# Reordering the start and the chunk loop of a fused attention, expert and dense kernel on one core: an early `w_out` slab, two-chunk turns, lagging rests and a softmax in four parts

## The chip, the core and the metric

The kernel runs on one core of a Trainium2 chip. TensorE multiplies matrices into PSUM banks, VectorE, ScalarE and GpSimd (POOL) work on tiles in SBUF (VectorE and ScalarE on PSUM too), and SyncE issues the transfers from and to HBM. Each engine runs its own instructions in their order and waits for the others by semaphores. The metric is the device time of one execution in microseconds; the number to predict is the median of the runs of the changed kernel. The kernel before took 355.84 us (median of three; 353.69 to 357.73).

## The reference

Three stages on 3072 tokens of width 512. The expert weights, `w_in` and `w_out` come as below; `w_in` and `w_out` are 64-bit floats in memory, which the kernel turns to 32-bit ones on the chip ("decoding").

```python
# 1. decayed linear attention in blocks, 8 heads of 64
intra = (q k^T * D) v;  inter = (q * lam_pow) kv_state;  out = intra + inter
# 2. soft mixture of experts: 32 slots, 8 experts of 4 slots
d = softmax(x @ phi, over tokens);  slot_input = d.T @ x
slot_out[e] = relu(slot_input[e] @ w1[e]) @ w2[e]
c = softmax(x @ phi, over slots);   x = c @ slot_out
# 3. dense stage, 512 -> 2048 -> 512
h = x @ w_in;  g = h - tanh(h);  return g @ w_out
```

## The kernel before, in words

**Attention and routing (to about 129 us).** A loop over 24 units (6 blocks of 128 positions, 4 batches) computes scores, values, the running state and the routing logits. Weight loads run beside it: `fill` (L171) issues the next half slab on SyncE whenever its ring has a free place. The rings are pools of 1 MB places: `a` has 3, `b` 12, `d` and `e` one each, `c` 4 (`RING`, L61). The letter of each of the 32 expert slabs stands in `RING_OF` (L62); all 16 slabs of `w_in` (`wi0` to `wi7`) and `w_out` (`wo0` to `wo7`) go to `a`, in the order wi0, wi1, wo0, wo1, wi2, wi3, wo2, wo3 and so on (`slabs`, L166). `freed` (L183) gives a place back when the last instruction that reads the slab has been issued.

**Experts (129 to 171 us).** For each expert `expert1` (L569) multiplies the slot inputs by w1, `expert_t` (L583) turns the result and VectorE copies it to `hz`, `expert2` (L595) of the expert before multiplies by w2. Among them the softmax over slots is made in two halves: `gate` (L625) turns the logits, `gate_v` (L632) does the softmax on VectorE and ScalarE, `parts` (L651) splits it in a rounded part and a rest; `gate_t` (L665) makes the six column blocks `c4`.

**Dense stage.** Because x = c @ slot_out has rank 32, h comes from M = slot_out @ w_in: `make_m(m)` (L729) makes the 512 columns of M that two `wi` slabs give, `put_m` (L739) lays them out as `ms` (TensorE, a ScalarE copy, a VectorE subtraction on 32 rows), `turn_m` (L749) gives `mt` with the mean of each column (TensorE, a VectorE copy). Both use one PSUM bank (7), except the first ones. There are 6 column blocks c of 512 tokens and 16 row blocks f of 128 features, so 96 chunks (c, f). For each chunk `d_of` (L773) multiplies on TensorE into one of three banks; `r_of` (L779) squares d on ScalarE into `s` and multiplies: on VectorE from PSUM (L790), or, for the chunks in `POOL_R` (L56), on POOL after a second ScalarE pass `e`. The result `r`, the "rest", stands for the cubic part of h - tanh(h). `product` (L794) multiplies the four 128-token parts of r by the rounded `w_out` block `wr` (`round_wo`, L759, ScalarE) and adds up over the f of a turn in four banks. `TURNS` (L51) lists the turns (c, first f, end f). `keep` (L800) empties the banks: at a first turn of c into `part` on ScalarE, at the second by a VectorE addition and a store. The first-order part of the result, a product of c4 with `qc`, comes from `linear_1` to `linear_3` (L822 to L869), which need all of M and of w_out; the second turn of each c adds it in its banks (L1014), except for c = 0 (`LATE`, L55), for which `late_linear` (L809) does it a chunk or more later by itself.

**Order.** The order is written out by hand. `decode_ops` (L102) makes a slab's three VectorE steps (L107, L110, L113), each on 1024 elements a partition for a 1 MB slab. The steps of `wi0` and `wi1` stand ahead of everything (L699); those of the other 14 slabs form the list `filler`, and in iteration n of the chunk loop (L983) `FILLER[n]` of them are issued, after `d_of(n + 3)` and `r_of(n + 3)` and ahead of the products of chunk n. In turns the products of the last two chunks are issued together. When a slab is done, `decoded` (L961) puts what follows on later iterations, by `DUE` (L58): `make_m` 1, `put_m` and `turn_m` 2, `round_wo` 2 iterations later. Before the loop stand `make_m(0)`, `put_m(0)`, `turn_m(0)`, the d and r of chunks 0 to 2, three steps (`wo0`) and its rounding (L947 to L982). `keep_warm` (L608) issues products whose result nobody reads.

Of the kernel before, what the change touches and what calls it, by code (L numbers as in the profile page):

```python
# [18 lines left out]
P = 128  # L19
# [29 lines left out]
WARM_MAIN = 2, 2  # L49

TURNS = [  # L51
    (0, 0, 4), (1, 0, 4), (2, 0, 4), (3, 0, 8), (4, 0, 8), (5, 0, 12), (0, 4, 16), (1, 4, 16),
    (2, 4, 16), (3, 8, 16), (4, 8, 16), (5, 12, 16),
]
LATE = 0  # L55
POOL_R = range(2, 48, 2)  # L56
FILLER = [3] + [1] * 16 + [1, 1, 0] * 5 + [1] * 20
DUE = 1, 2, 2  # L58
# [3 lines left out]
RING_OF = "a" * 3 + "b" * 12 + "de" + "c" * 4 + "a" * 3 + "b" * 7 + "a"  # L62
# [3 lines left out]
def tile_main(ctx, tc, qkv, lam, phi, w1, w2, w_in, w_out, out):  # L66
# [496 lines left out]
    with pool("exp") as ep:  # L563
# [109 lines left out]
        fill()  # L673
        for e in range(NE):
            hr = expert1(e)
            if e in (1, 2):
                parts()
            if e >= 1:
                expert2(e - 1)
            if e < 2:  # L680
                softmax = gate(e)
# [3 lines left out]
            if e < 2:  # L685
                parts = softmax()
# [52 lines left out]
    def put_m(m, bk=None):  # L739
        pp = bank(bk or MISC, [P, 4, P], "pp")  # L740
        for j in range(4):
            nc.tensor.matmul(pp[:, j], put[:, j], m_t[m], start=True, stop=True, skip_group_check=True)
# [4 lines left out]
            out=ms[64:96, sl], in0=pp[64:96], in1=ms[64:96, sl].bitcast(F32), op=ALU.subtract)  # L747

    def turn_m(m, bk=None):  # L749
        tp = bank(bk or MISC, [P, 4, NS + 1], "tp")  # L750
        nc.tensor.matmul(
            tp.rearrange("p j s -> p (j s)"), m_t.pop(m), tsel.rearrange("p j s -> p (j s)"),
            start=True, stop=True)
        nc.vector.tensor_copy(mt[:, 4 * m:4 * m + 4], tp)
        placed.update((2 * m, 2 * m + 1))
# [15 lines left out]
    d_t, r_t = {}, {}  # L771
# [28 lines left out]
    def keep(c, op, t, sl, lo, hi):  # L800
# [5 lines left out]
        if hi == NF and c != LATE:  # L806
            nc.sync.dma_start(out=out_v[c, :, t, sl], in_=pt)

    def late_linear(t):  # L809
        op = bank(MISC, [P, DM], "opl")  # L810
        pt = part_t[LATE][:, t]
        nc.tensor.matmul(op, c4[:, LATE, t * P:(t + 1) * P], qc, start=True, stop=True)
        nc.vector.tensor_tensor(out=pt, in0=op, in1=pt, op=ALU.add)
        nc.sync.dma_start(out=out_v[LATE, :, t], in_=pt)
# [289 lines left out]
```

## Time and profile before

| what | value |
|---|---|
| median of three runs | 355.84 us |
| lowest, highest | 353.69, 357.73 us |
| the profiled execution | 357.14 us, of it 355.3 us span from the first to the last instruction |
| granted TensorE clock, mean | 0.944 of full speed |
| TensorE, VectorE, ScalarE, POOL busy | 313.1, 213.4, 141.1, 116.6 us |
| moved by DMA | 81.06 MB |

Full speed of TensorE's clock is 2.4 GHz; 0.50 is its lower level, 1.2 GHz. TensorE's instructions are pipelined, so its rows overlap and a busy TensorE is not one at its peak; from start to start is the safer reading. "DVE" is VectorE, "ACT" ScalarE, "PE" TensorE, "PEld" its weight loads, "SPq" the queue of SyncE. Times in the profile count from the first instruction.

### The profile page before, as it was taken

How to read it: one execution, taken by the hardware profiler on the slowest of the kernel's cores; microseconds unless marked ns; L12 is line 12 of the kernel's file. 1: busy time of each engine (PE TensorE's matmuls, PEld its weight loads, DVE VectorE, ACT ScalarE, POOL GpSimd, SP SyncE). 2: the span in 40 equal slices, each digit the busy share in tenths (PEclk: the TensorE clock that was granted, in tenths of full speed). 3: DMA queues.
4: the chain of work that ended last, by engine and by line, in shares of the span. 5: the costliest groups of instructions: out<-in, count | busy, mean ns of one | idle time of the engine just before them, and what ended most of it. 6: DMA issues, size and time to landing. Idle time of an engine off the chain costs nothing.

```text
span 355.3 us, 7076 instructions
## 1 busy us (share of the span) xinstructions
PE 313.1 (88%) x2828; PEld 232.6 (65%) x2828; DVE 213.4 (60%) x347; ACT 141.1 (40%) x270; POOL 116.6 (33%) x154
## 2 busy tenths in 40 slices
PE   8499999999999998799837887789788989999993
PEld 8488898989788863344515654566565657787773
DVE  2326555555544336301678989767959598767773
ACT  2023323232323223222136867469457534353330
POOL 6117687759583031110012635135525100000000
PEclk9659999999999999999856999899989999999998
DMA  6858999999999999999636453535300003303324
GB/s 196 285 179 283 400 395 400 391 397 390 390 391 317 366 378 393 400 399 375 240 136 224 159 197 132 176 101 192 124 0 2 2 0 120 118 0 118 120 73 168
DMA packets 34197, 81.06 MB, mean 228 GB/s; under 512 B 3048, under 2 KB 4464, under 8 KB 34160
## 3 DMA queue, kind: packets, MB, share of 16 engines
q1 hardware_dynamic: 34160, 80.56, 61.8%
q8 instruction: 23, 0.38, 0.4%
q14 instruction: 14, 0.11, 0.1%
HBM read 74.25 MB, written 6.30 MB: 227 GB/s over the span
## 4 chain that ended last, share of the span: by engine, by line
PE 34%; DVE 27%; DMA 25%; ACT 5%; issue 4%; POOL 1%; SPq 1%; DVEq 0%; POOLq 0%; ACTq 0%
PE ops L797 11%; DMA qk<-in_qkv 7%; DMA w<-in_w 7%; DVE r L790 6%; DMA k<-in_qkv 5%; DVE part L805 4%; PE dps L777 4%; PE xp L297 3%; DVE wif L110 3%; DVE wif L113 3%; PE sc L278 2%; ACT s L784 2%; DVE wif L107 2%; DMA v<-in_qkv 2%; DMA wi<-in_w_in 2%
## 5 line engine op out<-in xcount | busy, mean ns | idle before, releaser
L797 PE MATMUL ops<-wr,r 128*128 128x512 f32 (+1 forms) x388 | 114.7, 411 | 8.4 <-ACT wr L762 6.4
L797 PEld LDWEIGHTS ops<-wr,r 128*128 128x128 f32 x388 | 74.8, 195 | 34.5 <-ACT wr L762 5.5
L784 ACT ACTIVATE s<-dps 128x512 f32<-128x512 f32 x96 | 56.5, 603 | 55.1 <-PE dps L777 51.6
L790 DVE SCALAR_TENSOR_TENSOR r<-dps,mt,s 128x512 fp32r<-128x512 f32 x73 | 53.8, 747 | 27.0 <-ACT s L784 26.9
L788 POOL TENSOR_TENSOR r<-e,s 128x512 fp32r<-128x512 f32 x23 | 37.5, 1634 | 79.3 <-ACT e L787 62.6
L777 PE MATMUL dps<-c,ms 128*128 128x512 f32 x96 | 40.2, 439 | 7.6 <-DVE r L790 6.6
L282 DVE TENSOR_TENSOR at<-sc,dtab 128x512 f32<-128x512 f32 x48 | 30.8, 686 | 17.1 <-DMA dtab<-zd 8.6
L247 POOL TENSOR_TENSOR qs<-qk,ql 128x512 f32<-128x512 f32 x20 | 25.5, 1273 | 24.2 <-DMA qk<-in_qkv 20.5
L297 PE MATMUL xp<-at,v 128*64 128x128 f32 x384 | 28.6, 291 | 4.6 <-DVE at L282 4.6
L315 DVE TENSOR_TENSOR st<-up,sd 64x256 f32<-64x256 f32 x32 | 13.5, 423 | 29.5 <-PE up L307 29.0
L301 ACT COPY xt<-xp 128x512 f32<-128x512 f32 x24 | 14.1, 586 | 39.3 <-PE xp L297 39.3
L337 ACT COPY xn<-xnp 128x512 f32<-128x512 f32 x24 | 14.1, 586 | 39.3 <-PE xnp L335 39.3
L777 PEld LDWEIGHTS dps<-c,ms 128*128 128x128 f32 x96 | 19.0, 200 | 16.1 <-DVE r L790 9.4
L278 PE MATMUL sc<-qk 64*128 64x128 f32 x384 | 28.8, 291 | 0.7 <-DMA qk<-in_qkv 0.7
L278 PEld LDWEIGHTS sc<-qk 64*128 64x128 f32 x384 | 24.1, 193 | 6.9 <-DMA qk<-in_qkv 3.4
L297 PEld LDWEIGHTS xp<-at,v 128*64 128x64 f32 x384 | 22.2, 143 | 8.2 <-DVE at L282 5.1
L254 POOL TENSOR_TENSOR kc<-k,dtab 128x512 f32<-128x512 f32 x20 | 21.2, 1060 | 18.8 <-PE up L307 11.5
L291 PE MATMUL xp<-qs,st 128*128 128x128 f32 x160 | 21.2, 276 | 0.0
L260 POOL TENSOR_TENSOR sd<-st,ql 64x256 f32<-64x256 f32 x32 | 19.8, 618 | 1.2
L598 PE MATMUL op<-w,hz 128*32 128x512 f32 x128 | 16.5, 595 | 3.5 <-DVE hz L591 3.5
L291 PEld LDWEIGHTS xp<-qs,st 128*128 128x128 f32 x160 | 19.5, 192 | 0.1
L335 PE MATMUL xnp<-cst,xt 128*128 128x128 f32 x96 | 16.2, 292 | 0.0
(188 smaller groups left out, 379.0 us busy)
## 6 DMA issues: line engine op xcount, KB each, us to landing
w<-in_w SPq DMA_DIRECT2D x64, 512.0 KB, 8.8
qk<-in_qkv SPq DMA_DIRECT2D x24, 512.0 KB, 7.8
wi<-in_w_in SPq DMA_DIRECT2D x16, 512.0 KB, 5.0
wo<-in_w_out SPq DMA_DIRECT2D x16, 512.0 KB, 3.4
v<-in_qkv SPq DMA_DIRECT2D x24, 256.0 KB, 6.8
out<-part SPq DMA_DIRECT2D x23, 256.0 KB, 2.2
k<-in_qkv SPq DMA_DIRECT2D x17, 256.0 KB, 8.5
dtab<-zd SPq DMA_DIRECT2D x2, 256.0 KB, 5.0
```

Of the source, the lines that this page charges most:

```text
L247: nc.gpsimd.tensor_tensor(out=qs_t[u], in0=qk_t[u][:, 0], in1=ql, op=ALU.mult)
L254: nc.gpsimd.tensor_tensor(out=kc_t[u], in0=k_t.pop(u).rearrange("p (h d) -> p h d", h=H), in1=kd, op=ALU.mult)
L260: nc.gpsimd.tensor_tensor(out=sd_t[u][sl], in0=st_t[b][sl, :, sl], in1=lb[sl].to_broadcast([DH, NP, DH]), op=ALU.mult)
L278: nc.tensor.matmul(sc[h2][:, p], qk[sl, 1, p], qk[sl, 0, p], start=True, stop=True)
L282: nc.vector.tensor_tensor(out=by_head(at_t[u], h2), in0=sc[h2], in1=by_head(dtab, h2), op=ALU.mult)
L291: nc.tensor.matmul(xp[:, p], st_t[b][:, p], qs_t[u][:, p], start=p == 0, stop=False, skip_group_check=True)
L297: nc.tensor.matmul(xp[h2 * DH:(h2 + 1) * DH, p], v[:, h * DH:(h + 1) * DH], at[:, h], start=c == 0 and p == 0, stop=True, skip_group_check ...
L777: nc.tensor.matmul(d_t[n], ms[:, f * P:(f + 1) * P], c4[:, c], start=True, stop=True)
L784: nc.scalar.activation(out=s, in_=d, func=AF.Square, scale=math.sqrt(1.0 / 3))
L788: nc.gpsimd.tensor_tensor(out=r_t[n], in0=e, in1=s, op=ALU.mult)
L790: nc.vector.scalar_tensor_tensor(out=r_t[n], in0=d, scalar=mt[:, f, NS:], in1=s, op0=ALU.add, op1=ALU.mult)
L797: nc.tensor.matmul(op, r_t[n][:, t * P:(t + 1) * P], wr_t[f // 2][:, f % 2, sl], start=first, stop=last)
```

## The change

- The last expert slab goes to ring `b` instead of `a`.
- The softmax over slots: half 0 is computed behind expert 0 and split behind expert 1, half 1 behind experts 2 and 3. Before, half 0 was computed behind expert 0, half 1 behind expert 1, and each was split behind `expert1` of the next one.
- The first two turns have 2 chunks instead of 4, and their second turns 14 instead of 12.
- The three steps of `wo0` are issued ahead of `turn_m(0)` and `put_m(0)`, `turn_m` comes ahead of `put_m` everywhere (in the loop a chunk ahead), and its rounding ahead of the first d. Two groups of two `keep_warm` products are added.
- `s_of(n + 3)` issues the squares (and `e`) where `r_of(n + 3)` did; the rest itself is `r_of(n + 2)`.
- POOL has the rests of the odd chunks 7 to 45 (20) instead of the even ones 2 to 46 (23).
- `FILLER` is another list: 15 steps in iterations 0 to 10, then three in four iterations, to iteration 42 (before: one in each up to 16, then two in three, then one in each, to iteration 41).
- `late_linear` goes; c = 0 gets its first-order part at the end of its second turn like the others.

```diff
-WARM_MAIN = 2, 2
+WARM_MAIN = 2, 2, 2, 2
 TURNS = [
-    (0, 0, 4), (1, 0, 4), (2, 0, 4), (3, 0, 8), (4, 0, 8), (5, 0, 12), (0, 4, 16), (1, 4, 16),
+    (0, 0, 2), (1, 0, 2), (2, 0, 4), (3, 0, 8), (4, 0, 8), (5, 0, 12), (0, 2, 16), (1, 2, 16),
     (2, 4, 16), (3, 8, 16), (4, 8, 16), (5, 12, 16),
 ]
-LATE = 0
-POOL_R = range(2, 48, 2)
-FILLER = [3] + [1] * 16 + [1, 1, 0] * 5 + [1] * 20
-DUE = 1, 2, 2
+POOL_R = range(7, 47, 2)
+FILLER = [3, 1, 1, 2, 1, 2, 1, 1, 1, 1, 1, 0] + [1, 1, 1, 0] * 8
+DUE = 1, 2, 3, 2
-RING_OF = "a" * 3 + "b" * 12 + "de" + "c" * 4 + "a" * 3 + "b" * 7 + "a"
+RING_OF = "a" * 3 + "b" * 12 + "de" + "c" * 4 + "a" * 3 + "b" * 8
...
+        softmax = []
         for e in range(NE):
             hr = expert1(e)
-            if e in (1, 2):
-                parts()
             if e >= 1:
                 expert2(e - 1)
             if e < 2:
-                softmax = gate(e)
+                softmax.append(gate(e))
...
             expert_t(e, hr)
-            if e < 2:
-                parts = softmax()
+            if e in (0, 2):
+                parts = softmax[e // 2]()
+            elif e in (1, 3):
+                parts()
...
+    def s_of(n):
+        s, e = tmp("s", bufs=3), None
+        nc.scalar.activation(out=s, in_=d_t[n], func=AF.Square, scale=math.sqrt(1.0 / 3))
+        if n in POOL_R:
+            e = tmp("e", bufs=2)
+            nc.scalar.activation(
+                out=e, in_=d_t[n], func=AF.Identity, bias=mt[:, chunks[n][1], NS:])
+        s_t[n] = s, e
     def r_of(n):
...
-        d = d_t.pop(n)
-        s = tmp("s", bufs=3)
+        d, (s, e) = d_t.pop(n), s_t.pop(n)
         r_t[n] = tmp("r", F32R, bufs=5)
-        nc.scalar.activation(out=s, in_=d, func=AF.Square, scale=math.sqrt(1.0 / 3))
-        if n in POOL_R:
-            e = tmp("e", bufs=2)
-            nc.scalar.activation(out=e, in_=d, func=AF.Identity, bias=mt[:, f, NS:])
+        if e is not None:
             nc.gpsimd.tensor_tensor(out=r_t[n], in0=e, in1=s, op=ALU.mult)
...
+    for _ in range(3):
+        done, step = filler.pop(0)
+        step()
+    turn_m(0, 4)
     put_m(0, 3)
-    turn_m(0, 4)
-    d_of(0)
-    d_of(1)
-    r_of(0)
-    r_of(1)
-    d_of(2)
-    r_of(2)
+    round_wo(0)
+    keep_warm(WARM_MAIN[2], 5)
+    for n in range(LA):
+        d_of(n)
+        s_of(n)
+    keep_warm(WARM_MAIN[3], 5)
+    for n in range(LA - 1):
+        r_of(n)
     def decoded(n, w, i):
         if w == "wi" and i % 2:
             at(n + DUE[0], lambda: make_m(i // 2))
-            at(n + DUE[1], lambda: put_m(i // 2))
             at(n + DUE[1], lambda: turn_m(i // 2))
+            at(n + DUE[2], lambda: put_m(i // 2))
...
-                for t in range(B):
-                    at(n + DUE[1] + 16 + t, lambda t=t: late_linear(t))
         elif w == "wo":
-            at(n + DUE[2], lambda: round_wo(i))
+            at(n + DUE[3], lambda: round_wo(i))
...
-    for _ in range(3):
-        done, step = filler.pop(0)
-        step()
-    round_wo(0)
     for n in range(NN):
...
         if n + LA < NN:
             d_of(n + LA)
-            r_of(n + LA)
+            s_of(n + LA)
+        if n + LA - 1 < NN:
+            r_of(n + LA - 1)
...
-                product(*s, n, f == lo, hi < NF or c == LATE)
-                if hi == NF and c != LATE:
+                product(*s, n, f == lo, hi < NF)
+                if hi == NF:
                     op, t, sl = s
                     nc.tensor.matmul(op, c4[:, c, t * P:(t + 1) * P], qc[:, sl], start=False, stop=True)
```

## Rows read from the trace of the kernel before

**Rows 1.** From the page: TensorE's busy tenths in 40 equal slices of the span (8.9 us each), and the clock that was granted to it in the same slices, in tenths of full speed.
```profile
PE   8499999999999998799837887789788989999993
...
PEclk9659999999999999999856999899989999999998
```

**Rows 2.** Busy time of each engine in four stages of the second half: stage (us from the span's start), its length, then PE, PEld, DVE, ACT and POOL busy us (instructions), granted clock as a share of full speed, busy share of the DMA rings, GB/s.
```profile
174.40:182.10 7.70, 5.74 (x42) 4.13 (x42) 2.29 (x4) 2.80 (x6) 0.00 (x0) 0.58 0.83 318
182.10:188.50 6.40, 1.39 (x4) 0.91 (x4) 4.72 (x5) 1.75 (x3) 1.52 (x1) 0.50 0.18 49
188.50:274.10 85.60, 70.13 (x353) 50.28 (x355) 71.07 (x75) 56.46 (x102) 34.92 (x22) 0.94 0.37 132
...
290.00:320.00 30.00, 29.48 (x124) 22.63 (x123) 23.12 (x40) 13.83 (x24) 0.00 (x0) 1.00 0.19 70
```

**Rows 3.** Who waited for whom between 188.5 and 274.1 us: waiting engine, group and line, releaser, us in total, times, longest us.
```profile
DVE r L790 <- ACT s L784: 10.2, 10, 2.3
...
DVE ms L746 <- ACT ms L745: 3.5, 2, 3.1
```

**Rows 4.** Timeline of TensorE behind 306 us, where it alone is the limit: start us, us, engine, line, operation, out<-in, count (and in brackets, in this and the later timelines, the idle time before it and what ended it). The first row is the first chunk of a turn.
```profile
306.40 1.98 PE L797 MATMUL ops<-wr,r 128*128 128x512 f32 x4
308.21 0.40 PE L777 MATMUL dps<-c,ms 128*128 128x512 f32 x1
308.45 1.08 PE L797 MATMUL ops<-wr,r 128*128 128x512 f32 x4
...
309.60 1.08 PE L797 MATMUL ops<-wr,r 128*128 128x512 f32 x4
```

**Rows 5.** Timeline of VectorE at the start of the last stage.
```profile
168.01 0.70 DVE L107 TENSOR_SCALAR wif<-wi 128x1024 uint32<-128x1024 uint32 x1 [1.28 <-DMA wi<-in_w_in]
...
173.13 1.23 DVE L113 SCALAR_TENSOR_TENSOR wif<-wi,wif 128x1024 uint32<-128x1024 uint32 x1
178.58 0.69 DVE L746 TENSOR_TENSOR ms<-pp,ms 32x512 fp32r<-32x512 f32 x1 [4.23 <-ACT ms L745]
...
180.79 1.41 DVE L790 SCALAR_TENSOR_TENSOR r<-dps,mt,s 128x512 fp32r<-128x512 f32 x2 [1.19 <-ACT s L784]
...
182.83 2.17 DVE L110 SCALAR_TENSOR_TENSOR wf<-wo,wf 128x1024 uint32<-128x1024 uint32 x1
...
188.54 0.68 DVE L107 TENSOR_SCALAR wf<-wo 128x1024 uint32<-128x1024 uint32 x1
```

**Rows 6.** Timeline of TensorE and ScalarE in the same stretch.
```profile
169.43 0.74 PE L612 MATMUL wp<-c 128*128 128x512 f32 x2
...
175.84 2.08 PE L742 MATMUL pp<-lt_all,put 128*128 128x128 f32 x8 [0.36 <-ACT lt_all L737]
...
177.71 0.65 PE L751 MATMUL tp<-tsel,lt_all 128*128 128x132 f32 x2
177.95 0.60 ACT L745 ACTIVATE ms<-pp 128x512 fp32r<-128x512 f32 x1 [2.17 <-PE pp L742]
...
180.16 1.57 ACT L784 ACTIVATE s<-dps 128x512 f32<-128x512 f32 x3 [1.61 <-PE dps L777]
...
186.29 1.06 ACT L762 ACTIVATE wr<-wf 128x1024 fp32r<-128x1024 f32 x1 [3.98 <-DVE wf L113]
...
187.40 2.07 PE L797 MATMUL ops<-wr,r 128*128 128x512 f32 x4 [5.01 <-ACT wr L762]
```

**Rows 7.** Stages around the landing of the first `w_in` slabs, with the columns of rows 2.
```profile
166.00:168.00 2.00, 2.00 (x19) 0.93 (x16) 0.19 (x1) 0.60 (x1) 0.00 (x0) 1.00 1.05 388
168.00:169.00 1.00, 1.00 (x8) 0.43 (x8) 0.95 (x2) 0.44 (x1) 0.00 (x0) 1.00 0.64 238
169.00:170.00 1.00, 1.00 (x6) 0.30 (x2) 0.97 (x1) 0.15 (x1) 0.00 (x0) 1.00 0.33 123
```

**Rows 8.** Timeline of SyncE, which issues the loads: first issue, us over which the issues of the row are spread, issues.
```profile
160.95 2.96 SPq L138 DMA_DIRECT2D wi<-in_w_in  x4
171.19 1.76 SPq L130 DMA_DIRECT2D wo<-in_w_out  x4
```

**Rows 9.** Timeline of TensorE among the experts.
```profile
146.66 0.64 PE L598 MATMUL op<-w,hz 128*32 128x512 f32 x4 [2.50 <-DVE hz L591]
```

**Rows 10.** VectorE's busy time between 188.5 and 274.1 us in the three lines of the decoding alone, one answer each, L107, L110 and L113 from the top: stage, its length, busy us (instructions), granted clock, DMA share, GB/s.
```profile
188.50:274.10 85.60, 13.21 (x13) 0.94 0.37 132
188.50:274.10 85.60, 18.89 (x13) 0.94 0.37 132
188.50:274.10 85.60, 20.54 (x13) 0.94 0.37 132
```

**Rows 11.** Timeline of TensorE and VectorE around the end of the linear part.
```profile
279.81 1.02 PE L857 MATMUL qr<-k,gsum 128*128 128x512 f32 x2
...
284.06 0.75 DVE L868 SCALAR_TENSOR_TENSOR qc<-s,ends,k 32x512 fp32r<-32x512 f32 x1
...
285.65 0.49 PE L777 MATMUL dps<-c,ms 128*128 128x512 f32 x1 [1.31 <-DVE r L790]
```

**Rows 12.** Timeline of TensorE at three places: eight output products at full clock, and a `d` product and eight output products behind an idle time of 3.45 us.
```profile
209.08 2.02 PE L797 MATMUL ops<-wr,r 128*128 128x512 f32 x8
...
223.53 0.79 PE L777 MATMUL dps<-c,ms 128*128 128x512 f32 x1 [3.45 <-DVE r L790]
...
224.12 3.25 PE L797 MATMUL ops<-wr,r 128*128 128x512 f32 x8
```

More of the change, by code (lines that the diff above doesn't have):

```diff
@@ L740, in put_m @@
         pp = bank(bk or MISC, [P, 4, P], "pp")
+        mm_ = m_t.pop(m)
         for j in range(4):
-            nc.tensor.matmul(pp[:, j], put[:, j], m_t[m], start=True, stop=True, skip_group_check=True)
+            nc.tensor.matmul(pp[:, j], put[:, j], mm_, start=True, stop=True, skip_group_check=True)
         pp = pp.rearrange("p j f -> p (j f)")
@@ L747, in put_m @@
             out=ms[64:96, sl], in0=pp[64:96], in1=ms[64:96, sl].bitcast(F32), op=ALU.subtract)
+        placed.update((2 * m, 2 * m + 1))
     def turn_m(m, bk=None):
@@ L751, in turn_m @@
         nc.tensor.matmul(
-            tp.rearrange("p j s -> p (j s)"), m_t.pop(m), tsel.rearrange("p j s -> p (j s)"),
+            tp.rearrange("p j s -> p (j s)"), m_t[m], tsel.rearrange("p j s -> p (j s)"),
             start=True, stop=True)
         nc.vector.tensor_copy(mt[:, 4 * m:4 * m + 4], tp)
-        placed.update((2 * m, 2 * m + 1))
     rounded = set()
@@ L769, in tile_main @@
     assert sorted(x[:2] for x in chunks) == [(c, f) for c in range(NC) for f in range(NF)]
-    d_t, r_t = {}, {}
+    d_t, s_t, r_t = {}, {}, {}
     def d_of(n):
@@ L805, in keep @@
             nc.vector.tensor_tensor(out=pt, in0=op, in1=pt, op=ALU.add)
-        if hi == NF and c != LATE:
+        if hi == NF:
             nc.sync.dma_start(out=out_v[c, :, t, sl], in_=pt)
[L809 to L814, printed above, removed]
     qc = main.tile([P, DM], F32R, name="qc")
@@ L963, in decoded @@
             at(n + DUE[0], lambda: make_m(i // 2))
-            at(n + DUE[1], lambda: put_m(i // 2))
             at(n + DUE[1], lambda: turn_m(i // 2))
+            at(n + DUE[2], lambda: put_m(i // 2))
             if i == NF // 2 - 1:
-                at(n + DUE[1] + 1, lambda: state.update(gt=linear_1()))
+                at(n + DUE[2] + 1, lambda: state.update(gt=linear_1()))
                 at(n + DUE[1] + 8, check_1)
@@ L970, in decoded @@
                 at(n + DUE[1] + 14, lambda: state.update(flag=check_3()))
-                for t in range(B):
-                    at(n + DUE[1] + 16 + t, lambda t=t: late_linear(t))
         elif w == "wo":
-            at(n + DUE[2], lambda: round_wo(i))
+            at(n + DUE[3], lambda: round_wo(i))
             if i == NF // 2 - 1:
-                at(n + DUE[2] + 1, lambda: state.update(qs=linear_2(state["gt"])))
-                at(n + DUE[2] + 3, lambda: linear_3(state["qs"]))
-    for _ in range(3):
-        done, step = filler.pop(0)
-        step()
-    round_wo(0)
+                at(n + DUE[3] + 1, lambda: state.update(qs=linear_2(state["gt"])))
+                at(n + DUE[3] + 3, lambda: linear_3(state["qs"]))
     for n in range(NN):
@@ L1010, in tile_main @@
                     product(*s, n - 1, f - 1 == lo, False)
-                product(*s, n, f == lo, hi < NF or c == LATE)
-                if hi == NF and c != LATE:
+                product(*s, n, f == lo, hi < NF)
+                if hi == NF:
                     op, t, sl = s
```

## The prediction

> **What bounds the kernel now.** I read the page first, for where TensorE is not busy or not at full clock. The reader is to see in [rows 1] that the dip in its busy row and that in its clock row sit in the same place, slices 20 to 22 (counted from 1), and that shallower ones follow up to slice 32. In time (a slice is 8.9 us) that is the stretch that begins where the expert weights are used up, at about 175 us. Then I cut that part into stages [rows 2]. From 290 us on TensorE is busy 29.48 of 30.00 us at full clock, so it alone bounds the tail. From 188.5 to 274.1 us TensorE is busy 70.13 of 85.60 and VectorE 71.07: the two take turns at waiting. From 174.4 to 188.5 neither is busy: VectorE works 2.29 + 4.72 us of 14.1, and TensorE runs at 0.58 and 0.50 of its clock, the lower level of 1.2 GHz. That is a chain, not a loaded engine. Who waits for whom in the middle stretch [rows 3] shows VectorE idle 10.2 us for ScalarE's squares (ten waits) and 3.5 us for `ms`.
>
> The floor of the later stretch is a chunk in TensorE's row: one `d` product and four output products, 1.15 us from start to start (309.60 less 308.45) [rows 4]. A first chunk of a turn takes 1.98 in place of 1.08 us for its products, 0.9 us more, as the bank has to be emptied.
>
> **The start (slab `wo0` while M is made).** VectorE ends the second `wi` slab at 174.36 us and then does nothing until the `ms` subtraction at 178.58, idle 4.23 us by the row; `wo0` is decoded only behind the first two rests, from about 182.2, where its second step runs beside POOL and takes 2.17 us; the first output product waits 5.01 us for `wr` and starts at 187.40, and the decode of `wo1` starts at 188.54 [rows 5, 6]. The change puts the three steps of `wo0` straight behind `wi1`: 0.70 + 1.23 + 1.23 = 3.16 us (the uncontended steps of the `wi` slabs), from 174.4 to 177.5, inside the hole. TensorE's side of the hole grows: `turn_m` now stands ahead of `put_m`, +0.65 us at the low clock. ScalarE's rounding of `wo0` (1.06 us) comes between its `ms` copy and the first square, a gap of 0.69 (VectorE's subtraction) + 0.89 (from its end at 179.27 to the first square at 180.16), so it is hidden; were it not, it costs at most 1.06. Two warm-up products of 0.74 us stand behind `put_m`, where TensorE waits 0.60 + 0.69 us for `ms`: hidden too; the other two stand between the third `d` and the fourth, which waits for a rest anyway. Before, the second rest ended at 182.2; now at 182.2 + 0.65 = 182.8; with the third rest (0.70, on POOL before) the decode of `wo1` starts at 183.5 in place of 188.54. Lead 5.0 us. Its condition is that `wo0` has landed by 174.4. Its load was issued at 171.19, when the last expert slab gave up its ring place, when the DMA rings had run dry: they were full until 168 us and then moved 1 us at 238 GB/s and 1 us at 123 GB/s, 0.36 MB, to finish `wi1` [rows 7, 8]. The change gives that expert slab a place in the other ring, so `wo0` (1.05 MB) follows `wi1` at 388 GB/s: 169.4 + 2.7 = 172.1 us. In time by 2.3 us.
>
> The same ring letter lets `wi0` be issued one expert earlier than `wi1`, where both were issued together at 160.95. The rings are full either way, so only the order can change: before, 0.36 of 1.05 MB was left when `wi0` was used at 168.01; if all of `wi1` stands behind it, `wi0` is there (1.05 - 0.36) / 388 GB/s = 1.8 us sooner. Against that, `wo0` may share the rings with `wi1` and hold it back by 0.9 us (172.1 less the 171.2 at which it is needed). I take 1.0 us gained, between -0.9 and 1.8: even issued together, `wi0` was there with a third of `wi1` still out. Lead at `wo1`: 6.0 us.
>
> **The softmax in four parts.** It removes waits of TensorE on `hz`, the longest of which is 2.50 us [rows 9]. The weights' DMA is full in that time and sets when `wi0` lands, so I count nothing, except that `so` is ready in time for the 1.0 us above; below nothing, TensorE then idles before M is made and its 1.07 us at full clock could become 2.1.
>
> **Two-chunk turns, the new filler list.** Turns 0 and 1 need only `wo0`, so `wo1` is wanted at chunk 6, not 2. M's second part is wanted at chunk 12, not 16; `put_m(1)` is issued at chunk 8 and the `d` of chunk 12 right behind it, so that one stall on `ms` stays (some 1.4 us of TensorE, under a VectorE that is later still). For the others `turn_m` no longer waits for the bank that `ms` holds.
>
> **Rests a chunk later.** All 39 decode steps from `wo1` on stay on VectorE, so what counts is how long it takes from the first to the last: before 188.5 to 274.1 (the third stage was cut at these two), 85.6 us, of it 71.1 busy and 14.5 idle [rows 2]. Rests: 23 instead of 20 up to chunk 44, +3 x 0.70 (two in 1.41 us [rows 5]) = +2.1. POOL's rests slow decode steps: 39 steps took 13.21 + 18.89 + 20.54 = 52.6 us, uncontended 13 x 3.16 = 41.1, so 11.5 [rows 10] over 22 POOL rests (chunks 4 to 46), 0.52 each; two fewer, -1.0. Idle: a rest now follows its square by one more VectorE turn, some 0.7 + 1.0 = 1.7 us, which covers eight of the ten waits whole. I leave 1.2 us of them, and 2.8 for `ms` and for the product that goes to `mt`: 4.0 in place of 14.5. Bounds: 0 and 14.5. Sum 85.6 + 1.1 - 10.5 = 76.2, from 182.5 (188.5 less 6.0) to 258.7 us. In both kernels the rest of chunk 44 precedes the last step, and TensorE stands at that chunk. TensorE's own floor to there: 45 x 1.15, six turn starts x 0.9, three M parts of some 2.5, 3 us of low clock at first: 67.7 from 182.8, 250.5 us. Only 8 us apart, so the two will still catch each other; I add 2 (between 0 and 8). At 260.7 TensorE is where it was at 274.1: lead 13.4 us.
>
> **No late turn any more.** Chunk set 0 ends at chunk 49 with its linear part, two chunks behind `linear_3`. From the end of `qr` (280.83) to the last piece of `qc` (284.06 + 0.75) took 4.0 us [rows 11]; between them TensorE now has two `d` and two output products, 0.9 us. It waits 3.1 us. After an idle of 3.45 us the eight products took 3.25 instead of 2.02 and the `d` ahead of them 0.79 instead of 0.40 [rows 4, 12]: 1.6 us of low clock more. Loss 4.7; bounds 0 (VectorE ahead) and 6. Of the waits for rests behind 274 us, the longest of them 1.31, about 1.0 goes. The four late additions are beside TensorE: nothing. From chunk 64 on nothing differs.
>
> **Sum.** 13.4 - 4.7 + 1.0 = 9.7 us sooner. The profiled execution took 357.14 us (span 355.3), the median is 355.84; from that, 346.1. I say 346.
>
> Beside a rest on POOL a decode step goes from 1.23 to 2.17 us [rows 5], 0.9 more, and the mean is 0.52 for each rest. The Trainium skill, "SBUF — State Buffer", section "Who interferes with whom", says the shared port pair is an exclusive lock: whichever of the two starts first holds it for the whole instruction and the other one blocks. By that each of the 19 remaining rests could cost VectorE its whole run in a denser VectorE stream; the trace bears out the blocking, but only as often as the mean says. It is the third rival.
>
> **Rivals.** (1) *Everything kept*: no catching each other (+2.0), no wait at chunk 49 (+4.7): 9.7 + 6.7 = 16.4, 339 us. For it: VectorE could be ahead by then. Against: `qc` hangs on a fixed chain. (2) *The waits only move*: the rest now reaches TensorE later in the order, and VectorE's 14.5 us idle comes back in other places: 6.0 - 1.1 - 4.7 + 1.0 = 1.2, 354.6 us. For: TensorE waits for rests already, 3.45 us at the longest [rows 12]. Against: the waits on the squares are short and many, as a lag cures. (3) *POOL costs twice as much*: 19 x 0.5 = 9.5 more, 355.6 us. (4) *The clock stays low*: two-chunk turns and rests on VectorE's pace leave TensorE in pieces. At 1.2 GHz a chunk costs 1.15 more and each M part 2.5. If half of chunks 0 to 44 run so, TensorE's floor grows by 0.5 x 45 x 1.15 less the 3 counted, plus 4: 27 us to 277, past VectorE's 259; it is then 3 us behind 274.1, and 4.7 - 1.0 more at chunk 49: 6.7 slower, 362.5 us. It decides once some 40% of those chunks run so, a mean granted clock of some 0.72 from 183 us on. For: 0.50 from 182.1 to 188.5, and the slow eight products. Against: 0.94 in the long stretch, with stalls as long [rows 2].
>
> **How the numbers follow.** Forecast 0.65 (own range 342 to 351), (1) 0.12, (2) 0.10, (3) 0.07, (4) 0.06. Under 1%, some 3.6 us, a measurement of this kernel can't tell from no change. Faster by over 1%: forecast and (1), 0.77; within: (2) and (3), 0.17; slower: 0.06. The range 339 to 354 takes in (1) and the near half of (2) and leaves out the rest, 0.18.
>
> **What would show it.** Right: the first output product at about 183 us, `wo1` decoded from 182 to 184; waits of rests on squares under 3 us between there and the last decode step, which ends at 256 to 263; a TensorE wait of some 3 us for `qc` before the first linear product; the last 31 chunks as before. Wrong: a wait of VectorE for `wo0` at 174; decode steps above 1.5 us on average; a granted clock under 0.8 after 190; a last decode step after 268.

## The result and the profile after

The changed kernel takes 346.62 us in the median (342.61 to 348.54, four runs) beside 356.78 us for the kernel before (353.69 to 360.61, four runs). The ratio is 0.9653, with a 95% interval of 0.9569 to 0.9737; it leaves out the executions that are over 1.5% above the fastest of their kernel (348.54 and 348.34 us of the changed kernel, 360.61 of the other), so it is not the quotient of the medians. The forecast was 346.0 us, between 339 and 354, with 0.77 for faster. The two profiled executions lie 8.6 us apart (357.14 and 348.54 us; spans 355.3 and 346.8). That of the changed kernel is the slowest of its four, at a mean granted clock of 0.943. A second profile of the same kernel (341.30 us, span 339.5, clock 0.962; the control under Experiments) is set beside it where the two differ.

TensorE's busy tenths and its granted clock in 40 slices of the span, of the changed kernel:

```profile
PE   8699999999999999998577689999759699999993
...
PEclk9769999999999999999859989999898969999998
```

The dip that stood in slices 20 to 22 [rows 1] is shallower in the busy row (5 at the lowest, 3 before), and the clock is back by slice 22. A new dip stands in slices 30 to 32: busy 5, 9 and 6, with the clock at 8 in slice 31 and at 6 in slice 33. It is looked at below.

Stages of the changed kernel, cut at the same events as before, with the columns of rows 2: while the second `w_in` slab is decoded; up to the first step of `wo1`; from there to the last decode step.

```profile
168.50:174.90 6.40, 1.37 (x12) 0.83 (x11) 6.26 (x7) 0.27 (x1) 0.00 (x0) 0.66 0.66 246
174.90:184.20 9.30, 7.65 (x48) 5.43 (x49) 5.90 (x8) 3.96 (x7) 0.00 (x0) 0.68 0.75 260
184.20:264.30 80.10, 67.10 (x349) 49.75 (x348) 70.67 (x78) 55.74 (x101) 30.79 (x21) 0.94 0.37 132
```

VectorE now works 5.90 of the 9.30 us ahead of `wo1`. The third stage is 80.1 us long in place of 85.6, with 70.67 us of VectorE in place of 71.07 [rows 2]: nearly the same work with 9.4 us of idle time instead of 14.5. In the second profile the same stage is 78.2 us long:

```profile
179.00:257.20 78.20, 65.37 (x348) 48.51 (x348) 73.01 (x78) 55.59 (x100) 30.54 (x21) 0.96 0.38 135
```

There VectorE is busy for 73.0 us and idle for 5.2.

Who waited in that third stage (waiting group, releaser, us in total, times, longest):

```profile
PE dps L779 <- DVE r L797: 7.2, 6, 3.7
...
DVE mt L757 <- PE tp L754: 4.9, 3, 3.0
...
DVE ms L748 <- ACT ms L747: 2.5, 3, 1.2
...
DVE r L797 <- ACT s L783: 1.3, 4, 0.5
```

The waits of rests on squares have gone from 10.2 to 1.3 us [rows 3]. TensorE waits 7.2 us for rests, the longest 3.7 (below). VectorE's waits for `ms` are 2.5 us, and those for the product that goes to `mt` have grown to 4.9, from 1.8 before. In the second profile the squares cost 1.2 us, `ms` 0.4 and `mt` 2.8:

```profile
DVE mt L757 <- PE tp L754: 2.8, 2, 1.5
```

The largest difference between the two profiles is at the last part of M. TensorE waits 1.79 us for a decode step ahead of it in both. In the first profile the granted clock is 0.79 behind that wait (244 to 252 us), and in the second it stays at 1.00 (237 to 245 us). The output products two rows on, in the first and in the second profile:

```profile
246.90 1.91 PE L804 MATMUL ops<-wr,r 128*128 128x512 f32 x4
```

```profile
240.90 1.09 PE L804 MATMUL ops<-wr,r 128*128 128x512 f32 x4
```

VectorE then waits 3.0 us for the product that goes to `mt` in the first profile and 1.5 in the second.

Timeline of TensorE at the first chunk of a late turn and at the one behind it:

```profile
300.36 1.31 PE L804 MATMUL ops<-wr,r 128*128 128x512 f32 x4
...
301.74 1.10 PE L804 MATMUL ops<-wr,r 128*128 128x512 f32 x4
```

The first chunk takes 1.31 us, 1.98 before [rows 4]. Nothing in the forecast said so.

Timeline of VectorE at the start of the last stage:

```profile
168.51 0.69 DVE L106 TENSOR_SCALAR wif<-wi 128x1024 uint32<-128x1024 uint32 x1 [5.25 <-DMA wi<-in_w_in]
...
173.62 1.22 DVE L112 SCALAR_TENSOR_TENSOR wif<-wi,wif 128x1024 uint32<-128x1024 uint32 x1
174.76 0.69 DVE L106 TENSOR_SCALAR wf<-wo 128x1024 uint32<-128x1024 uint32 x1
...
176.74 1.23 DVE L112 SCALAR_TENSOR_TENSOR wf<-wo,wf 128x1024 uint32<-128x1024 uint32 x1
...
182.28 2.07 DVE L797 SCALAR_TENSOR_TENSOR r<-dps,mt,s 128x512 fp32r<-128x512 f32 x3 [1.22 <-ACT s L783]
184.27 0.68 DVE L106 TENSOR_SCALAR wf<-wo 128x1024 uint32<-128x1024 uint32 x1
```

The steps of `wo0` stand directly behind those of `wi1`, without a wait, from 174.76 us. The three rests follow at 182.28 and the first step of `wo1` at 184.27; before it was at 188.54 [rows 5].

Timeline of TensorE there:

```profile
171.87 0.64 PE L734 MATMUL mp__2315<-wif,so 128*32 128x128 f32 x4 [2.64 <-DVE wif L112]
174.90 1.92 PE L734 MATMUL mp__2315<-wif,so 128*32 128x128 f32 x28 [2.39 <-DVE wif L112]
...
177.79 1.92 PE L744 MATMUL pp<-lt_all,put 128*128 128x128 f32 x8
...
184.09 2.02 PE L804 MATMUL ops<-wr,r 128*128 128x512 f32 x8
```

The first output products start at 184.09 us, before at 187.40 with a wait of 5.01 [rows 6]. The M products take 1.92 us and stand behind a wait of 2.39: TensorE had ended the experts, went idle and lost its full clock (granted 0.66 in the first of the stages above). Before, the granted clock was 1.00 from 168.0 to 174.4 us, and they took 1.07 us:

```profile
174.41 1.07 PE L733 MATMUL mp__2315<-wif,so 128*32 128x128 f32 x28 [0.94 <-DVE wif L113]
```

VectorE's busy time in the decode lines, from the first step of `wo1` to the last (stage, length, busy us and instructions, clock, DMA share, GB/s):

```profile
184.20:264.30 80.10, 12.05 (x13) 0.94 0.37 132
184.20:264.30 80.10, 18.37 (x13) 0.94 0.37 132
184.20:264.30 80.10, 20.16 (x13) 0.94 0.37 132
```

Together 50.6 us for the 39 steps; less 41.1 that is 9.5 over 20 POOL rests, 0.47 each. Before it was 52.6 us and 0.52 [rows 10]. In the second profile it is 53.1 us and 0.60. 15 of the 39 steps take longer than they do alone, in the second profile 17, and each of these overlaps a rest on POOL.

Timeline of TensorE and VectorE at the end of chunk set 0:

```profile
271.95 1.02 PE L857 MATMUL qr<-k,gsum 128*128 128x512 f32 x2
...
276.20 0.75 DVE L868 SCALAR_TENSOR_TENSOR qc<-s,ends,k 32x512 fp32r<-32x512 f32 x1
...
277.10 0.76 PE L1015 MATMUL ops<-qc,c 128*128 128x512 f32 x1 [3.20 <-DVE qc L868]
...
277.66 1.05 PE L804 MATMUL ops<-wr,r 128*128 128x512 f32 x2
```

The wait for `qc` is 3.20 us, and the pairs of output products behind it take 1.05 us each, at the lower clock. The same rows of a later turn take 0.62. The second profile has the same wait of 3.20 us and the same 1.05 behind it.

One wait was not foreseen. Timeline of VectorE and TensorE around `linear_1`:

```profile
255.36 1.30 DVE L826 TENSOR_TENSOR g<-mt 128x16 f32<-128x16 f32 x1
...
258.36 0.69 DVE L839 TENSOR_TENSOR lt_all<-lt_all,g 128x512 f32<-128x512 f32 x1
...
259.76 0.79 PE L779 MATMUL dps<-c,ms 128*128 128x512 f32 x1 [3.70 <-DVE r L797]
...
260.35 1.91 PE L804 MATMUL ops<-wr,r 128*128 128x512 f32 x4
```

`linear_1` holds VectorE from 255.36 to 259.05 us between two rests, and TensorE waits 3.70 us for the next rest and then multiplies at the lower clock. This and the wait for `qc` are the new dip of slices 30 to 32.

**Where the time went.** The first `wi0` step starts between 163.7 and 168.5 us in the profiles of this study, also in kernels with the same instructions up to there. So the stages are counted from that step. All numbers are differences of starts and ends in the timelines, us:

| kernel | first `wo1` step | last decode step ends | last product ends |
|---|---|---|---|
| before | 20.5 | 106.0 | 181.9 |
| changed, first profile | 15.8 | 95.8 | 172.8 |
| changed, second profile | 15.2 | 93.4 | 170.2 |
| lag undone | 16.4 | 102.6 | 181.1 |
| before with the lag alone | 17.0 | 97.0 | 174.3 |
| early slab undone | 19.2 | 100.5 | 177.6 |
| old turns | 15.4 | 93.6 | 168.1 |
| old softmax places | 13.8 | 91.9 | 167.6 |
| old ring letter | 16.1 | 93.7 | 170.7 |
| late linear part back | 15.8 | 95.8 | 174.5 |
| warm-up | 13.8 | 93.8 | 170.9 |
| `linear_1` apart | 15.5 | 91.7 | 166.3 |
| late part, `linear_3` spread | 15.3 | 93.5 | 168.3 |
| the last three together | 13.8 | 90.4 | 166.0 |

Of the 9.0 us between the kernel before and the first profile 4.8 come at the start and 5.5 in the decode stretch; 1.3 are given back behind it, where the wait for `qc` and the low clock take more than the turn starts return. With the second profile it is 11.6 us: 5.3, 7.3 and 1.0 given back. One profile differs from another of the same kernel by up to 2.6 us here.

### The profile page after: what moved, and what is told of

Read it like the earlier page. It is cut to its first block, busy times and chain, and to the rows that moved or that the text cites. A ratio compares the mean times of both kernels' runs of the same rounds, so it can differ in the third digit from the quotient of the medians.

```text
span 346.8 us, 7051 instructions
## 1 busy us (share of the span) xinstructions
PE 311.8 (90%) x2832; PEld 235.0 (68%) x2832; DVE 211.1 (61%) x346; ACT 139.6 (40%) x267; POOL 109.5 (32%) x151
## 4 chain that ended last, share of the span: by engine, by line
PE 44%; DMA 31%; DVE 15%; issue 3%; POOL 2%; ACT 2%; SPq 1%; DVEq 0%; POOLq 0%; ACTq 0%
PE ops L804 19%; DMA w<-in_w 11%; DMA qk<-in_qkv 10%; PE dps L779 5%; DMA k<-in_qkv 5%; DMA wi<-in_w_in 3%; PE xp L296 3%; DVE r L797 3%; DVE wif L109 2%; PE sc L277 2%; DVE wif L112 2%; PE ops L1015 2%; DVE wif L106 2%; PE xnp L334 1%; DVE wf L112 1%
## 5 line engine op out<-in xcount | busy, mean ns | idle before, releaser
L804 PE MATMUL ops<-wr,r 128*128 128x512 f32 (+1 forms) x388 | 112.9, 410 | 0.8 <-POOL r L795 0.8
L804 PEld LDWEIGHTS ops<-wr,r 128*128 128x128 f32 x388 | 76.0, 197 | 21.3 <-ACT part L810 1.8
L797 DVE SCALAR_TENSOR_TENSOR r<-dps,mt,s 128x512 fp32r<-128x512 f32 x76 | 55.8, 746 | 17.4 <-ACT s L783 16.7
L795 POOL TENSOR_TENSOR r<-e,s 128x512 fp32r<-128x512 f32 x20 | 29.7, 1484 | 80.4 <-ACT e L786 73.8
L573 PE MATMUL hp<-w,si 128*32 128x256 f32 x256 | 16.0, 383 | 1.3 <-DMA w<-in_w 1.3
L812 DVE TENSOR_TENSOR part<-ops,part 128x512 f32<-128x512 f32 (+1 forms) x25 | 15.4, 661 | 2.3 <-PE ops L1015 2.3
```

Of the source, the lines that this page charges most:

```text
L795: nc.gpsimd.tensor_tensor(out=r_t[n], in0=e, in1=s, op=ALU.mult)
L797: nc.vector.scalar_tensor_tensor(out=r_t[n], in0=d, scalar=mt[:, f, NS:], in1=s, op0=ALU.add, op1=ALU.mult)
L804: nc.tensor.matmul(op, r_t[n][:, t * P:(t + 1) * P], wr_t[f // 2][:, f % 2, sl], start=first, stop=last)
```

## Experiments

Each kernel was timed beside the kernel before on the same chip; the ratio is to that. The intervals are some 0.6% wide to either side, 2 us, so a difference of two edits is settled only from some 3 us on. The first is the changed kernel without an edit.

> The changed kernel again, as the reference for the runs beside it. 342 to 348 us, ratio to the kernel before 0.957 to 0.974.

Measured: 343.77 us, ratio 0.9688 (0.9624 to 0.9753). The kernels without the lag, without the early slab and with the late part ran on the same chip as this one; the others ran on two other chips and are held against it by their ratios. The new `FILLER` list, POOL's other chunks, the order of `turn_m` and `put_m` and the two new groups of `keep_warm` were not taken back by themselves; what they are worth is not shown.

**The lag of the rests.**

```diff
-        if n + LA - 1 < NN:
-            r_of(n + LA - 1)
+        if n + LA < NN:
+            r_of(n + LA)
```

> Only the lag of the rests undone: the rest of chunk n + 3 in iteration n, right behind its square; all else as changed. My account (the lag takes VectorE's waits for squares out of the decode stretch and lets a turn's bank be emptied one rest sooner): VectorE waits some 8 to 10 us for squares again between the first wo1 step and the last decode step (1.3 with the lag), the first chunk of a late turn takes 1.98 us again (1.31 with it), and the time is 5 to 9 us above the control. Rival (VectorE's waits only move, and the gain is all from the early slab and the two-chunk turns): within 1.5 us of the control.

Measured: 353.92 us, ratio 0.9964 (0.992 to 1.0007): 10.2 us above the control (9.8 by the ratios), next to none of the gain left. From the first step of `wo1` to the last decode step (181.6 to 267.8 us, 86.2 long) the waits for squares are back:

```profile
DVE r L797 <- ACT s L783: 7.1, 7, 2.2
```

and so is the slow first chunk of a turn:

```profile
302.81 1.97 PE L804 MATMUL ops<-wr,r 128*128 128x512 f32 x4
```

My account holds in both places; 7.1 us of waits is under the 8 to 10 that I wrote, and the effect on the time is larger than I wrote. Beside the second profile of the changed kernel, `wo1` comes 1.2 us later (a fourth rest stands ahead of it), the stretch is 7.9 us longer, and what stands behind it 1.8. The wait for `qc` is 3.20 us here too.

The lag alone in the kernel before:

> The kernel before with the lag alone: squares in iteration n for chunk n + 3, the rest of chunk n + 2. My account (the lag works by itself: VectorE's 10 us of waits for squares go, and a late turn's first chunk starts 0.67 us sooner): 8 to 10 us below the kernel before. Rival (it needs the early slab and the other turns to have something to decode or multiply in the time that it frees): 0 to 4 us below.

Measured: 348.36 us, beside 356.26: ratio 0.9832 (0.9776 to 0.9887), between 4 and 8 us with the interval. My account wrote 8 to 10, the rival up to 4; the value lies between them. The waits for squares are 2.9 us, but VectorE waits 5.0 for `ms`, which is made a chunk later than `turn_m` only in the full change:

```profile
DVE ms L746 <- ACT ms L745: 5.0, 3, 2.3
...
DVE r L795 <- ACT s L781: 2.9, 3, 2.0
```

The turn start is the short one, with nothing else of the change present:

```profile
297.74 1.32 PE L802 MATMUL ops<-wr,r 128*128 128x512 f32 x4
```

So the short turn starts come from the lag. The order of the instructions says why: a rest that comes a chunk later stands behind the four additions of `keep` on VectorE, not ahead of them, so that the banks are free sooner. The traces show it. With the lag the additions start 0.81 us behind the first linear product of a turn (312.98), and without it 1.46 us behind (300.29). Timeline of VectorE in the changed kernel and in the one without the lag:

```profile
313.79 2.47 DVE L812 TENSOR_TENSOR part<-ops,part 128x512 f32<-128x512 f32 x4
```

```profile
301.75 2.47 DVE L812 TENSOR_TENSOR part<-ops,part 128x512 f32<-128x512 f32 x4
```

**The early slab.** The three steps and the rounding of `wo0` go back behind the first rests.

```diff
-    for _ in range(3):
-        done, step = filler.pop(0)
-        step()
     turn_m(0, 4)
     put_m(0, 3)
-    round_wo(0)
...
         r_of(n)
+    for _ in range(3):
+        done, step = filler.pop(0)
+        step()
+    round_wo(0)
```

> Only the decoding and rounding of the first w_out slab put back behind the first rests; ring, lag, turns and all else as changed. My account (VectorE's chain sets the end of the decode stretch): the first wo1 step is 3 to 4 us later than in the changed kernel, the last decode step too, and the time is 3 to 4.5 us above the control. Rival (TensorE's own floor is so near that most of it is made up): 0 to 1.5 us above.

Measured: 347.49 us, ratio 0.9759 (0.9698 to 0.982), 3.7 us above the control (2.5 by the ratios). Timeline of its VectorE (first step of `wi0`, of `wo0`, of `wo1`):

```profile
167.06 0.69 DVE L106 TENSOR_SCALAR wif<-wi 128x1024 uint32<-128x1024 uint32 x1 [5.59 <-DMA wi<-in_w_in]
...
182.46 0.68 DVE L106 TENSOR_SCALAR wf<-wo 128x1024 uint32<-128x1024 uint32 x1
...
186.24 0.68 DVE L106 TENSOR_SCALAR wf<-wo 128x1024 uint32<-128x1024 uint32 x1
```

From `wi0` to `wo1` it takes 19.2 us, 15.8 and 15.2 in the two profiles of the changed kernel: 3.4 to 4.0 us later, as my account says. The time lies nearer to the account (3 to 4.5 us) than to the rival (TensorE makes it up, 0 to 1.5), but the intervals overlap, so the time alone does not rule the rival out.

**The parts that cost or give little.** Old turns, old places of the softmax, old ring letter, each alone in the changed kernel:

```diff
-    (0, 0, 2), (1, 0, 2), (2, 0, 4), ..., (0, 2, 16), (1, 2, 16),
+    (0, 0, 4), (1, 0, 4), (2, 0, 4), ..., (0, 4, 16), (1, 4, 16),
...
+            if e in (1, 2):
+                parts()
...
+            if e < 2:
+                parts = softmax()
...
-RING_OF = ... + "a" * 3 + "b" * 8
+RING_OF = ... + "a" * 3 + "b" * 7 + "a"
```

> The changed kernel with the old turns (4 chunks in the first two), all else as changed. My account (VectorE sets the pace there, so the order of the chunks is nearly free; the wait for qc shrinks as chunk set 0 ends two chunks later): 1.5 us below to 1.5 above the control. Rival (TensorE then waits for the second w_out slab and cannot make it up): 2 to 4 us above.

Measured: 343.17 us, ratio 0.9724 (0.9659 to 0.979).

> The changed kernel with the softmax in its old two places, all else as changed. My account (full DMA rings set when the first w_in slab lands, so the waits among the experts cost nothing, and a TensorE that ends the experts later is still at full clock for M): 1.5 us below to 0.5 above the control; the M products take 1.07 us in place of 1.92. Rival (the waits on hz count): 2 to 4 us above.

Measured: 342.06 us, ratio 0.9738 (0.9669 to 0.9807). The M products run at full clock, and the wait before them is short:

```profile
172.64 1.07 PE L733 MATMUL mp__2315<-wif,so 128*32 128x128 f32 x28 [1.14 <-DVE wif L112]
```

> The changed kernel with the old ring letter of the last expert slab, all else as changed. wo0 is issued when the last expert product is, some 3 us sooner than in the kernel before because the experts end sooner. My account (it then still lands by the time its decoding starts, so the letter alone is worth little): 0 to 1.5 us above the control. Rival (VectorE waits for wo0): 2 to 4 us above, with a wait of the first wo0 step for its DMA.

Measured: 344.54 us, ratio 0.9779 (0.9707 to 0.9851). VectorE does not wait for `wo0` with the old letter either:

```profile
164.99 0.69 DVE L106 TENSOR_SCALAR wif<-wi 128x1024 uint32<-128x1024 uint32 x1 [4.97 <-DMA wi<-in_w_in]
...
170.10 1.22 DVE L112 SCALAR_TENSOR_TENSOR wif<-wi,wif 128x1024 uint32<-128x1024 uint32 x1
171.24 0.69 DVE L106 TENSOR_SCALAR wf<-wo 128x1024 uint32<-128x1024 uint32 x1
```

The timeline of SyncE in it says why:

```profile
164.47 4.56 SPq L129 DMA_DIRECT2D wo<-in_w_out  x4
```

`wo0` is issued 0.5 us ahead of the first `wi0` step, where before it was 3.2 us behind it [rows 5, 8]. The last expert product ends 0.6 us ahead of the first `wi0` step here (at 164.43), and 3.1 us behind it before, so the ring place of the last expert slab comes free sooner. Beside the new softmax places `wo0` comes in time without the letter.

All three intervals overlap the control's and that of the changed kernel. By the medians the three stand 0.6 and 1.7 us below the control and 0.8 above it, by the ratios 1.3, 1.8 and 3.2 above. So the times don't settle the rivals (2 us and more). For the ring letter the wait that its rival needs is not in the trace. None of the three parts is shown to help. What the softmax edit does can be seen, though: the experts end sooner, and TensorE waits for `w_in` and comes to M at half clock. From `wi0` to `wo1` the old places take 13.8 us, the new ones 15.8 and 15.2. The two-chunk turns have a price too: with the old turns TensorE doesn't wait for `qc` but 2.49 us for a rest (at 274.87), and the linear products behind it take 0.39 us each, 0.63 to 0.77 in the changed kernel. From the last decode step to the end it takes 74.5 us, in the two profiles of the changed kernel 77.1 and 76.8.

**The late linear part.**

```diff
-                product(*s, n, f == lo, hi < NF)
-                if hi == NF:
+                product(*s, n, f == lo, hi < NF or c == LATE)
+                if hi == NF and c != LATE:
...
+                for t in range(B):
+                    at(n + DUE[1] + 16 + t, lambda t=t: late_linear(t))
```

> Only the late linear part of chunk set 0 put back (four products and additions by themselves behind chunk 52, no wait for qc at chunk 49); all else as changed. My account: the TensorE wait of 3.2 us and the low clock behind it (about 1.7 us) go, the four additions are beside TensorE: 3.5 to 5 us below the control. Rival (VectorE is behind there anyway, so the time is spent waiting for rests): 0 to 1 us below.

Measured: 348.12 us, ratio 0.9784 (0.9729 to 0.9839), 4.4 us above the control (3.4 by the ratios) where I expected 3.5 to 5 below. The account fell. Timeline of VectorE and TensorE there:

```profile
274.79 0.69 DVE L872 TENSOR_TENSOR qc<-qr,s 32x512 fp32r<-32x512 f32 x1 [2.73 <-ACT s L868]
...
276.75 0.75 DVE L876 SCALAR_TENSOR_TENSOR qc<-s,ends,k 32x512 fp32r<-32x512 f32 x1
...
278.34 0.55 PE L780 MATMUL dps<-c,ms 128*128 128x512 f32 x1 [2.49 <-DVE r L798]
...
279.59 2.59 PE L805 MATMUL ops<-wr,r 128*128 128x512 f32 x4 [0.71 <-DVE part L813]
```

TensorE needs no `qc`, and still it waits 2.49 us for a rest and 0.71 for an addition, together the 3.20 that it waited for `qc`. VectorE stands in its queue for the ScalarE half of `linear_3` (2.73 us) and then does the four operations of `qc`; the next rests and the additions that empty the banks come only behind them. So the wait hangs on what is queued on VectorE, and not on `qc` itself. Why the kernel is slower than the control, and not just as fast, is not shown. To test the account, the VectorE operations were moved away from the ScalarE ones (the edit also issues the late part two iterations and `check_3` eight iterations later, and puts a ScalarE result in another buffer):

```diff
+                at(n + DUE[3] + 3, lambda: state.update(q=linear_3(state["qs"])))
+                at(n + DUE[3] + 5, lambda: state.update(l=linear_3a(*state["q"])))
+                at(n + DUE[3] + 6, lambda: linear_3b(*state["l"]))
```

> The changed kernel with the late linear part of chunk set 0 back (as in the run before with that alone) and linear_3's four VectorE operations moved two and three iterations behind its ScalarE ones, so that VectorE does not stand in its queue for them. My account, formed from the run before (TensorE did not wait for qc as such there but for the rests and additions queued behind the qc operations on VectorE): no TensorE wait over 1 us behind qr, 3 to 5 us below the changed kernel and 6 to 8 below the late part alone. Rival (the late part costs by its own products and additions): as the late part alone.

Measured: 342.42 us, ratio 0.9676 (0.9616 to 0.9737): 5.7 us below the late part alone, each beside its own runs of the kernel before (by the ratios 1.1%, 3.8 us; the two intervals just overlap). The waits of TensorE behind `qr`:

```profile
272.67 2.29 PE L805 MATMUL ops<-wr,r 128*128 128x512 f32 x4 [0.73 <-DVE part L813]
...
276.68 0.50 PE L780 MATMUL dps<-c,ms 128*128 128x512 f32 x1 [0.57 <-DVE r L798]
...
278.76 0.50 PE L780 MATMUL dps<-c,ms 128*128 128x512 f32 x1 [0.65 <-DVE r L798]
```

None is over 1 us, as the account says; the other moves of this edit are not told apart from it. Against the changed kernel it is within the interval, not the 3 to 5 us below that I expected.

**The cold start of M and `linear_1`.**

```diff
+    keep_warm(18)
     make_m(0)
```

> The changed kernel with 18 more products that nobody reads ahead of the first M, in the time in which TensorE waits for the w_in slabs. My account (TensorE comes cold to M because it ends the experts some 5 us before the slabs are decoded): the 28 M products take 1.07 us in place of 1.92 and what hangs on them starts 1.5 to 2.5 us sooner behind the first w_in step; 1 to 2.5 us below the changed kernel. Rival (VectorE or the rings set the start anyway): within 0.7 us.

Measured: 342.83 us, ratio 0.9654 (0.959 to 0.9718). The M products take 1.07 us and `wo1` starts 13.8 us behind `wi0`, 1.4 to 2.0 sooner than in the two profiles of the changed kernel. But the last decode step comes 93.8 us behind it, against 95.8 and 93.4 in the two profiles of the changed kernel. A gain of the expected size is not shown.

```diff
-        nc.vector.tensor_tensor(out=u, in0=b3, in1=b3, op=ALU.mult)
+        nc.gpsimd.tensor_tensor(out=u, in0=b3, in1=b3, op=ALU.mult)
...
+                at(n + DUE[2] + 3, lambda: linear_1a(state["g"][0]))
+                at(n + DUE[2] + 4, lambda: state.update(gt=linear_1b(state["g"][1])))
```

> The changed kernel with linear_1 taken apart: its six small operations on POOL, its two large ones on VectorE, two and three iterations later. My account (a run of 3.7 us on VectorE between two rests starves TensorE): the TensorE wait of 3.7 us there shrinks under 1.5, and the time falls by 2 to 4.5 us. Rival (VectorE is the limit there, so only the 2.3 us that leave it count, less what POOL slows): 0 to 2 us.

Measured: 341.02 us, ratio 0.9638 (0.9579 to 0.9697). The longest wait of TensorE for a rest there is now

```profile
257.84 0.50 PE L779 MATMUL dps<-c,ms 128*128 128x512 f32 x1 [2.54 <-DVE r L797]
```

2.54 us in place of 3.70, not under 1.5. The decode stretch is 76.2 us long, the shortest of the study. The median lies under the control's, but the intervals overlap.

All three edits together (the late part with `linear_3` spread, the warm-up, `linear_1` apart):

> The three edits together: 18 more warm-up products, linear_1 taken apart, and the late linear part with linear_3 spread. If the three waits are separate, 6 to 11 us below the changed kernel, a ratio of 0.935 to 0.955 to the kernel before. Rival (each gives its time back at the next one, since VectorE's work up to the last decode step is the limit): 2 to 4 us below.

Measured: 339.70 us (336.85 to 342.01), ratio 0.9596 (0.9543 to 0.965). It has the lowest median of the study and lies below the kernel before by more than its interval. It does not reach the 0.935 to 0.955 of separate waits; the rival's 2 to 4 us is nearer, and against the changed kernel's own ratios (0.9653, 0.9688) the intervals overlap.

## Why the prediction was right

**The start.** The lead of `wo1` without the ring term was put at 5.0 us. Counted from the first `wi0` step it is 4.8 in the first profile and 5.3 in the second, and taking the early slab away costs 3.4 to 4.0 us at `wo1` and 2.5 to 3.7 in the time. `wo0` had landed in time, as worked out. The cover named for the rounding and the warm-up products held.

**The ring letter's 1.0 us** failed. From the first expert product to the first `wi0` step it takes 38.3 us before (129.71 to 168.01) and 38.4 and 40.0 in the two profiles of the changed kernel: `wi0` doesn't come sooner. The three profiles with the old letter have 38.0, 38.3 and 38.6. The sum took it that the part of `wi1` that had gone ahead of `wi0` would go behind it. In both kernels the second half of `wi0` lands 2.7 us after the last half of an expert slab (167.89 after 165.17, now 168.38 after 165.67), and the rings moved 408 GB/s from 168 to 169 us where they moved 238 before [rows 7]. So more was left behind `wi0`, and it came no sooner for that. Why, no run here shows. And the loss that stood beside it as a possibility came: M's products at the low clock, 1.92 us. The old softmax places and the warm-up both take 1.4 to 2.0 us off the way to `wo1`, so the sum has a gain here where there was none, and a loss beside it that it left at nothing. No run shows that loss in the time beyond the intervals.

**The lag** is the heart of the change, and its step in the sum held where it was argued: 1.3 and 1.2 us of waits for squares left in the two profiles, 1.2 predicted. The kernel without the lag and the one with the lag alone say the same from both sides. The stretch was put at 76.2 us and 2 for the two engines catching each other; it took 80.0 us in the first profile and 78.2 in the second. For `ms` and `mt` 2.8 us were left, and 7.4 came in the first profile, of them 4.9 for `mt`, and 3.2 in the second. VectorE's copy to `mt` stands in its queue for a TensorE product, TensorE stands for the last decode step of a `w_in` pair (1.79 us ahead of M's last part), and in the first profile the clock behind that wait is low. The 2 us were meant for this: too small for the first profile, and the size of the second.

**POOL** slowed the decode steps by 0.47 us for each rest in the first profile and by 0.60 in the second, 0.52 predicted. The third rival, twice that price, is out; over all profiles of the study it is 0.45 to 0.64.

**Chunk 49.** 3.1 us predicted, 3.20 measured in both profiles. The clock behind it was priced at 1.6 us and cost some 2: the linear turn's end took 4.4 us (277.10 to 281.50) where the next one took 2.3, and behind the same wait in the kernel with `linear_1` apart, where the granted clock was 1.00, it took 2.4. That was nearly the right number from the right rows, but a reason one step short: with `qc` out of its way TensorE waited just as long, for a rest and an addition that stand behind the chain in VectorE's queue.

**From chunk 64 on** "nothing differs" was wrong. The four turn starts (chunks 64, 76, 84 and 92) are some 0.67 us shorter each; the first product of chunk 64 stood 6.0 us sooner (300.36 against 306.40 [rows 4]), the last product ended 8.5 sooner. The lag moved a rest behind `keep`, and the sum left out what it was moved past.

So 9.7 us were predicted on the profile. In the first profile the misses cancel. Against the sum the way to `wi0` lost 1.5 us (0.5 later instead of 1.0 sooner), the start 0.2, the decode stretch 1.9 (5.5 gained where the sum had 7.4 after the 2 set aside), and behind it 2.4 were won (1.3 given back in place of 4.7 - 1.0): -1.2 in all, 8.5 us between the two spans. In the second profile start and stretch came as summed (5.3 and 7.3 us for 5.0 and 7.4), and 1.0 was given back in place of 3.7: 11.6 us from `wi0` on, where the sum without its ring term has 8.7.

So the mechanism was right in the start and in the stretch. The sum had a ring term that is not there, and it left out the turn starts, some 2.5 us. That the median of four lies within 1 us of the forecast is luck: the ratios of both measurements (0.9653 and 0.9688) stand for a gain of 11 to 12 us, not 9.7. The signs given as times (`wo1` at 182 to 184 us, the last decode step at 256 to 263) were missed by 0.3 and 1.3 us in the first profile; they hang on when `wi0` comes, and so test little.

## What to carry to other kernels

An instruction that waits for another engine should stand in its queue behind work that is ready: here one place of lag between a square and what uses it was worth more than any other part that was tested, and alone it was worth half of the gain. When an instruction is moved past others in its queue, ask on both sides: what it stops holding up (the additions that free a turn's banks) is as much a term as what it waits for. A wait that another engine shows for a value may be a wait for all that is queued in front of it: here taking the value out of the way left a wait of the same 3.20 us, and with that work spread out in the queue no wait was over 1 us.

## What was not expected of the hardware

A faster stage cost TensorE its clock. The experts ended sooner, 0.8 us ahead of the first `wi0` step in place of 3.1 us behind it, and in the wait for the slabs the granted clock fell: 0.66 over 168.5 to 174.9 us, 1.00 in the same stage before. With eighteen products that nobody reads it stayed at 1.00 in that stage (1.07 us for M's products), and `wo1` came 1.4 to 2.0 us sooner. And the same wait can cost it in one execution and not in another: behind 1.79 us ahead of M's last part the granted clock was 0.79 in one profile of the changed kernel and 1.00 in the other.

The way to the first `wi0` step, a stretch with DMA rings that are full, differs by up to 4.8 us between profiles of kernels with the same instructions up to there (163.7 to 168.5 us). Parts of the last stage are thus only comparable when they are counted from an event at its start.
